# A prologue reordered: x and tables ahead of the weights, a mantissa converted on ScalarE, more of stage a between the two halves

## The chip, the cores and the metric

The kernel runs on one core of one Trainium2 chip. The metric is the device time of one execution in microseconds; the figure for a kernel is the median of several runs. A core has a matrix engine (TensorE, PE; its weight loads are PEld), VectorE (DVE), ScalarE (ACT), GpSimd (POOL), a sync engine (SP) that issues DMAs, and 16 DMA engines that all queues share.

## The reference

A Fourier layer, then a three-way maxout feed-forward layer, on x of 8 x 3072 x 256 (float32); the expert weights w1, w2, w3 (256 x 768) and w_out (768 x 256) come as float64.

```python
X = np.fft.rfft(x, axis=1)
Yr = X.real @ w_r - X.imag @ w_i + b_r
Yi = X.real @ w_i + X.imag @ w_r + b_i
Y = soft_threshold(Yr, 0.01) + 1j * soft_threshold(Yi, 0.01)
y = np.fft.irfft(Y, n=3072, axis=1).astype(np.float32).reshape(24576, 256)
h = np.maximum(np.maximum(y @ w1, y @ w2), y @ w3)
return (h @ w_out).astype(np.float32)
```

## The kernel before

The transform of 3072 points is split into 96 x 32. For each of the 8 batches, **stage a** multiplies a quad of x (`load_x`, `split_x`, `stage_a`; eight quads q to a batch, two matmuls pa each) by a 96-point table and writes the result, through tiles named aq, to a DRAM tile `a_d`. Twelve **blocks** k follow: `load_a` reads two rows of `a_d`, `stage_b` does the 32-point transform (px), `stage_w` multiplies by the complex weights (py) and adds the bias, a soft threshold comes next (uf, t), `finish_w` takes the maximum, `stage_q` does the first half of the inverse transform (pz) and writes zs to the DRAM tile `z_d`. Eight **chunks** c to a batch then read a piece of `z_d` (`load_z`, zq), split it into two float16 parts (`split_z`: zh on ScalarE, zl on VectorE), finish the inverse (`inverse`: pi, then yh and yl) and run the experts in six **slots** f: three `up` products (pu, each 6 float16 matmuls, combined by c on ScalarE and VectorE, h on VectorE, split into hh) and one `down` product (pd).

Batch 0 runs ahead of everything with float32 matmuls and on its own: eight quads of stage a, a loop over k from -3 to 12 with a hand-written plan of the weight work, and then the experts start. From there on the work of later batches is put between the slots of the experts by a list of positions in slots (`at`, `run_until`). Idle matmuls on zeros (`idle_matmuls`) fill PE's waits in the prologue.

The expert weights arrive as float64 and must become two float16 parts each. class `Weights` does that: `load` brings a pair of parts, `largest` takes the maximum of the high words, `scale` makes a power of two, and `phases` converts one part in three steps: exponent (a mask on VectorE, a Relu on ScalarE, L352 and L355), combine (four operations on VectorE, L359 to L367) and finish (the high part on ScalarE, two operations on VectorE, L126, L127 and L373). `w_up` has twelve parts of 128 x 384, `w_dn` six of 128 x 256. The plan of the loop takes the first six parts of `w_up` and three of `w_dn`; the others are `units`, of which `pump` moves each running one by a phase and starts one more. Pumps stand at k = 9 to 12 and five after each slot of the first chunk. `split_fft_weights` takes the maxima of the FFT weights and of the bias, makes their scales and splits them into float16 (L271 to L296), in program order after slot 2 of the first chunk; `largest_x` does not exist yet, the maxima of x (mxx, L444) are in `split_x`.

The program is ordered at build time: each engine gets one fixed list of instructions, chosen among those whose inputs should be there, the earlier in the program first. `tc.issue_after(ins)` adds an edge: what is traced inside it stands behind `ins` on that engine's list. `raw_tile` gives one of eight large buffers, `ff_tile` one of eight PSUM banks in turn, `quad_tile("aq")` one of two.

## Time and profile before

| | |
|---|---|
| runs | 2041.36, 2042.45, 2044.10 us; median 2042.45 |
| profiled execution | 2041.44 us, of which the span of the trace 2039.6 us |
| PE busy | 2016.9 us (99%) |
| PEld, DVE, ACT, POOL busy | 1413.9, 1447.3, 1032.3, 24.3 us |
| PE's part of the chain that ended last | 89%; DMA 4%, DVE 4% |

A busy PE includes its idle matmuls and the time at a lower granted clock. The chain is followed back from the last instruction to what released each step.

### The profile page before, as it was taken

The page shows a single profiled execution, that of the slowest core. Times are in us where ns is not written, and L with a number is a line of the kernel's source. Part 1 is how long each engine was busy: PE and PEld are TensorE (multiplying, and loading weights), DVE is VectorE, ACT ScalarE, POOL GpSimd, SP SyncE. Part 2 cuts the span into 40 slices and gives each one's busy share as a digit, 9 for nine tenths or more (in the row PEclk, how much of TensorE's full clock was granted, in tenths as well). Part 3 has the DMA queues.
Part 4 walks back from the last instruction along what each step waited for, and adds up shares of the span by engine and source line. Part 5 has one row for each costly group of instructions (what it writes and reads, how often), then busy time and mean ns, then how long its engine had stood idle before and what let it go on. Part 6 is the DMA issues. An engine that isn't in the chain of part 4 may idle for free.

```text
span 2039.6 us, 40089 instructions
## 1 busy us (share of the span) xinstructions
PE 2016.9 (99%) x15836; PEld 1413.9 (69%) x15836; DVE 1447.3 (71%) x2813; ACT 1032.3 (51%) x2050; POOL 24.3 (1%) x81
## 2 busy tenths in 40 slices
PE   8999999999999999999999999999999999999999
PEld 4756776677776777677776777767777677776666
DVE  3997886678766877668776777767876677755544
ACT  4756554455544554445554555545554455533333
POOL 1000000000000000000000000000000000000000
PEclk9999999999999999999999999999999999999999
DMA  9455542434333442434434344243441423211100
GB/s 312 149 160 140 141 119 86 119 99 124 93 103 84 120 115 72 125 80 123 105 95 113 81 120 104 80 117 98 109 111 47 117 73 100 66 53 32 40 24 24
DMA packets 199535, 207.74 MB, mean 102 GB/s; under 512 B 20131, under 2 KB 177827, under 8 KB 199251
## 3 DMA queue, kind: packets, MB, share of 16 engines
q1 hardware_dynamic: 138371, 129.20, 24.8%
q10 hardware_dynamic: 59744, 72.11, 11.1%
q0 software_dynamic: 1232, 3.87, 0.6%
q8 instruction: 124, 2.03, 0.4%
q14 instruction: 64, 0.52, 0.1%
HBM read 87.40 MB, written 75.50 MB: 80 GB/s over the span
## 4 chain that ended last, share of the span: by engine, by line
PE 89%; DMA 4%; DVE 4%; ACT 1%; issue 1%; SPq 0%; ACTq 0%; DVEq 0%
PE pu L159 17%; PE pu L160 17%; PE pu L161 17%; PE pd L161 6%; PE pd L160 6%; PE pd L159 6%; PE py L159 3%; PE py L161 3%; PE py L160 3%; PE px L586 2%; DMA ab<-a_d 1%; PE pa L161 1%; PE pa L160 1%; PE pa L159 1%; DMA zq<-z_d 1%; PE pi L161 1%
## 5 line engine op out<-in xcount | busy, mean ns | idle before, releaser
L159 PE MATMUL pu<-yh,wuh 128*128 128x384 f16 x2304 | 751.1, 326 | 6.0 <-ACT c L814 3.2
L160 PE MATMUL pu<-yl,wuh 128*128 128x384 f16 x2304 | 750.6, 326 | 0.9 <-DVE yl L154 0.7
L161 PE MATMUL pu<-yh,wul 128*128 128x384 f16 x2304 | 750.7, 326 | 0.0
L153 ACT ACTIVATE hh<-h 128x384 f16<-128x384 f32 x384 | 200.4, 522 | 530.8 <-DVE h L820 529.1
L817 DVE TENSOR_TENSOR c<-pu,c 128x384 f32<-128x384 f32 x384 | 211.9, 552 | 180.5 <-ACT c L814 93.7
L161 PEld LDWEIGHTS <-wul 128*128 128x128 f16 x2304 | 225.2, 98 | 150.9 <-issue 2.0
L159 PEld LDWEIGHTS <-wuh 128*128 128x128 f16 x2304 | 225.4, 98 | 130.5 <-issue 11.7
L160 PEld LDWEIGHTS <-wuh 128*128 128x128 f16 x2304 | 225.5, 98 | 130.0 <-issue 11.5
L161 PE MATMUL pd<-woh,hh 128*128 128x256 f16 x1152 | 313.7, 273 | 0.2 <-DVE ebf L294 0.2
L160 PE MATMUL pd<-wol,hh 128*128 128x256 f16 x1152 | 313.9, 273 | 0.0
L159 PE MATMUL pd<-woh,hh 128*128 128x256 f16 x1152 | 313.9, 273 | 0.0
L154 DVE SCALAR_TENSOR_TENSOR hh<-h,hh 128x384 f16<-128x384 f32 x384 | 213.1, 555 | 122.1 <-ACT hh L153 121.7
L814 ACT ACTIVATE c<-pu 128x384 f32<-128x384 f32 x384 | 185.8, 484 | 142.2 <-PE pu L161 123.4
L820 DVE TENSOR_TENSOR h<-pu,c 128x384 f32<-128x384 f32 x384 | 212.3, 553 | 57.9 <-PE pu L161 50.6
L159 PE MATMUL py<-wch,tt 128*128 128x256 f16 x504 | 137.4, 273 | 0.0
L161 PE MATMUL py<-wch,tt 128*128 128x256 f16 x504 | 137.3, 273 | 0.0
L160 PE MATMUL py<-wcl,tt 128*128 128x256 f16 x504 | 137.3, 272 | 0.0
L160 PEld LDWEIGHTS <-hh 128*128 128x128 f16 x1152 | 112.7, 98 | 33.4
L159 PEld LDWEIGHTS <-hh 128*128 128x128 f16 x1152 | 112.7, 98 | 33.4
L849 ACT ACTIVATE o<-pd,s1u 128x256 f32<-128x256 f32 x191 | 82.6, 466 | 82.2 <-PE pd L161 41.0
L161 PEld LDWEIGHTS <-hh 128*128 128x128 f16 x1152 | 112.7, 98 | 13.6 <-DVE ebf L294 0.5
L154 DVE SCALAR_TENSOR_TENSOR zl<-zq,s0u,zh 96x1024 f16<-96x1024 f32 (+1 forms) x65 | 81.9, 1262 | 31.8 <-ACT zh L153 31.8
(204 smaller groups left out, 2686.9 us busy)
## 6 DMA issues: line engine op xcount, KB each, us to landing
z_d<-zs ACTq DMA_DIRECT2D x96, 256.0 KB, 2.2
out_dram<-o ACTq DMA_DIRECT2D x190, 128.0 KB, 2.1
zq<-z_d SPq DMA_DIRECT2D x63, 384.0 KB, 4.1
xq<-in_x_dram SPq DMA_DIRECT2D x58, 384.0 KB, 4.1
a_d<-aq ACTq DMA_DIRECT2D x56, 384.0 KB, 3.3
ab<-a_d SPq DMA_DIRECT2D x84, 256.0 KB, 3.9
ab<-ab SPq DMA_DIRECT2D x336, 64.0 KB, 2.1
vb<-vb SPq DMA_DIRECT2D x308, 64.0 KB, 2.4
```

Source lines behind the costliest of these rows:

```text
L153: nc.scalar.activation(out=hi, in_=src, func=AF.Copy, scale=scale)
L154: later(lambda: nc.vector.scalar_tensor_tensor(out=lo, in0=src, scalar=scale, in1=h, op0=ALU.mult, op1=ALU.subtract))
L159: nc.tensor.matmul(o, lh, rh, start=start, stop=False, **kw)
L160: nc.tensor.matmul(o, lh, rl, start=False, stop=False, **kw)
L161: st["mm"] = nc.tensor.matmul(o, ll, rh, start=False, stop=stop, **kw)
L586: nc.tensor.matmul(pv[:, h, :, g // 2, g % 2], ah[:, g // 2, g % 2, h * P:(h + 1) * P], mb_sb[:, i, 4 * kb + g].rearrange("p (c m) -> p c ...
L814: nc.scalar.activation(out=c1, in_=p, func=AF.Copy)
L817: nc.vector.tensor_tensor(out=c1, in0=p, in1=c1, op=ALU.max)
L820: nc.vector.tensor_tensor(out=h32, in0=p, in1=st["c1"], op=ALU.max)
L849: nc.scalar.activation(out=o, in_=pd[t], func=AF.Copy, scale=st[b, "su"][1])
```

## The change

The order of loads in the prologue: x first, then two blocks of the table `mb_f`, and only behind the first read of `a_d` the FFT weights, the other blocks, the bias, `qf` and `id_sb` (on SP's queue, where they were on POOL's), then the expert weights, each one step of k later. `phases` works on a pair of parts at once and in four steps: the mantissa word goes through a ScalarE Relu (scale 2^-20, bias 1), the low word is added and the result multiplied by the power of two, so that VectorE has six operations for what took seven. The scales of the FFT weights move to k = 0 of the loop, their split stays after slot 2 but behind an edge. Quads 8 to 12 (before: 8 and 9) of x are loaded in the loop and go through stage a before the first inverse; their maxima are put at positions 1 to 3 of the slots. The pumps after the loop, the maxima and the split stand behind edges (`quiet`). Idle matmuls: 34 and 4 in place of 32 and 16.

```diff
+    EARLY = NCH + 5
 def load_fft_weights():
-        rows = [b.rearrange("(o d) -> o d", o=1) for b in (b_r, b_i)]
-        nc.gpsimd.dma_start(out=qf, in_=mq[:, 0:2])
-        for j in range(2):
-            for c in range(2):
-                nc.gpsimd.dma_start(
-                    out=bias[64 * c:64 * c + 64, j, :], in_=rows[c].broadcast_to([64, D])
-                )
-        nc.gpsimd.dma_start(out=bias[96:97, 1, :], in_=rows[0])
+    def load_tables():
+        rows = [b.rearrange("(r o d) -> r o d", r=1, o=1) for b in (b_r, b_i)]
+        for c in range(2):
+            nc.sync.dma_start(out=bias[64 * c:64 * c + 64], in_=rows[c].broadcast_to([64, 2, D]))
+        nc.gpsimd.dma_start(out=bias[96:97, 1:2], in_=rows[0])
+        nc.sync.dma_start(out=qf, in_=mq[:, 0:2])
+        nc.sync.dma_start(out=id_sb, in_=ident)
...
             def exponent():
-                e = x_tile("xh").bitcast(U32)[:, 0:width]
-                t["g"] = g = x_tile("xl").bitcast(U32)[:, 0:width]
+                g = x_tile().rearrange("p a b -> p (a b)")[:, 0:pair * width].bitcast(U32)
+                t["g"] = g = g.rearrange("p (k v) -> p k v", k=pair)
                 nc.vector.tensor_scalar(
-                    out=e, in0=hw, scalar1=0x7FF00000, scalar2=None, op0=ALU.bitwise_and
+                    out=g, in0=hw, scalar1=0x7FF00000, scalar2=None, op0=ALU.bitwise_and
                 )
-                nc.scalar.activation(out=g, in_=e, func=AF.Relu, scale=8.0, bias=ebias)
+                nc.scalar.activation(out=g, in_=g, func=AF.Relu, scale=8.0, bias=ebias)
             def combine():
...
                 nc.vector.tensor_scalar(
-                    out=hw, in0=hw, scalar1=12, scalar2=9, op0=ALU.logical_shift_left,
-                    op1=ALU.logical_shift_right,
+                    out=hw, in0=hw, scalar1=0xFFFFF, scalar2=None, op0=ALU.bitwise_and
                 )
-                nc.vector.tensor_tensor(out=hw, in0=hw, in1=g, op=ALU.bitwise_or)
+                nc.scalar.activation(out=m, in_=hw, func=AF.Relu, scale=2.0**-20, bias=ones)
+
+            def join():
                 nc.vector.scalar_tensor_tensor(
-                    out=r, in0=lw, scalar=2.0**-52, in1=g.bitcast(F32), op0=ALU.mult, op1=ALU.mult
+                    out=m, in0=lw, scalar=2.0**-52, in1=m, op0=ALU.mult, op1=ALU.add
                 )
+                nc.vector.tensor_tensor(out=m, in0=m, in1=t["g"].bitcast(F32), op=ALU.mult)
             def finish():
-                split_scaled(hi, m, m, self.sc)
-                nc.vector.scalar_tensor_tensor(
-                    out=lo, in0=r, scalar=self.sc, in1=m, op0=ALU.mult, op1=ALU.add
-                )
+                split_scaled(hi, lo, m, self.sc)
...
 def load_x(q):
-        with tc.issue_after(st["ld"].ins) if q >= NCH + 2 else nullcontext():
-            if 2 <= q < NCH:
+        with tc.issue_after(st["ld"].ins) if q >= EARLY else nullcontext():
+            if 2 <= q < NCH or NCH + 2 <= q < EARLY:
                 xq = raw_tile("xr")[0:N1, 0:NQ * D]
+    def largest_x(q, i, xp):
+        b, q4 = divmod(q, NCH)
+        with tc.issue_after(quiet[0]) if q < EARLY else nullcontext():
+            nc.vector.tensor_reduce(
+                out=batch(b, "x")[0:N1, 2 * q4 + i:2 * q4 + i + 1], in_=xp, axis=AX.X,
+                op=ALU.max, apply_absolute_value=True,
+            )
 def split_x(q):
+            if q >= EARLY:
+                largest_x(q, i, xp)
+            elif b:
+                at(1 + q4 / 2, lambda u: largest_x(*u), (q, i, xp))
...
-    load_first_blocks(0)
-    fft_weights = load_fft_weights()
+    load_first_blocks(0, 2)
...
-    idle_matmuls(32)
-    nc.gpsimd.dma_start(out=id_sb, in_=ident)
+    idle_matmuls(34)
     def prepare(w, n):
-        phase(w, n)
-        phase(w, n)
+        for _ in range(3):
+            phase(w, n)
-    for n in range(12):
-        if n % 2 == 0:
-            planned(-3 + n // 2, w_up.load, n)
+    for n in range(0, 12, 2):
+        planned(-2 + n // 2, w_up.load, n)
         planned(-2 + n // 2, w_up.largest, n)
-    for n in range(6):
-        planned(-1 + n, prepare, w_up, n)
+    for n in range(0, 6, 2):
+        planned(n, prepare, w_up, n)
         planned(5 + n // 2, phase, w_up, n)
...
         with tc.issue_after(st["ld"].ins):
+            if k == -3:
+                fft_weights = load_fft_weights()
+                load_first_blocks(2, 4)
+            if k == -2:
+                load_tables()
+            if k == 0:
+                scale_fft_weights(fft_weights)
+                split_scaled(*(t.rearrange("p a b -> p (a b)") for t in (qh, ql, qf)), Q_SCALE)
...
-            if k in (7, 8):
+            if 7 <= k < 12:
                 load_x(NCH + k - 7)
             if k == 9:
-                units += [(w_up, n) for n in range(6, 12)] + [(w_dn, n) for n in range(3, 6)]
-            if k >= 9:
+                units += [(w_up, n) for n in (6, 8, 10)] + [(w_dn, n) for n in (3, 4)]
+            if k in (9, 10):
                 pump()
-    for q in (NCH, NCH + 1):
+    with tc.issue_after(st["late"].ins):
+        for c, v in enumerate((b_r, b_i)):
+            row = v.rearrange("(o d) -> o d", o=1)
+            nc.gpsimd.dma_start(out=bias_ri[:, c], in_=row.broadcast_to([P, D]))
+    quiet = st["power"].ins, st["zs"].ins
+    def pumps(n):
+        with tc.issue_after(quiet[0]), tc.issue_after(quiet[1]):
+            for _ in range(n):
+                pump()
+    pumps(1)
+    for q in range(NCH, EARLY):
         split_x(q)
         stage_a(q)
-    idle_matmuls(16)
+    idle_matmuls(4)
     load_z(0, 0)
     split_z(0, 2)
     y = inverse(0, 0)
+    quiet = st["low"].ins, st["zs"].ins
...
-                    for _ in range(5):
-                        pump()
+                    pumps(5)
                     if f == 2:
-                        split_fft_weights(fft_weights)
+                        with tc.issue_after(quiet[0]):
+                            split_fft_weights(fft_weights)
```

Here `st["power"]` is the last operation of `power`, `st["zs"]` the last zs and `st["low"]` the last low part that `split_later` made with a scale.

## Rows read from the trace of the kernel before

**Rows 1.** The page's first part: busy time of PE, share of the span, instructions.

```profile
PE 2016.9 (99%) x15836; PEld 1413.9 (69%) x15836; DVE 1447.3 (71%) x2813; ACT 1032.3 (51%) x2050; POOL 24.3 (1%) x81
```

**Rows 2.** Busy time by stretch: the stretch in us from the span's start, its length, busy us (and instructions) of PE, PEld, DVE, ACT and POOL, granted PE clock, share of the 16 DMA engines, GB/s.

```profile
5.10:22.10 17.00, 15.37 (x36) 5.39 (x36) 1.11 (x2) 9.33 (x17) 4.73 (x10) 1.00 1.03 280
...
31.90:97.20 65.30, 64.20 (x313) 52.91 (x314) 60.42 (x151) 41.89 (x80) 0.96 (x3) 0.97 0.66 226
97.20:112.70 15.50, 12.71 (x61) 6.17 (x60) 14.35 (x40) 9.36 (x17) 0.00 (x0) 0.89 0.59 186
112.70:141.30 28.60, 27.39 (x177) 16.21 (x177) 28.12 (x76) 17.98 (x37) 0.00 (x0) 1.00 0.41 124
...
165.00:2039.60 1874.60, 1863.08 (x15072) 1314.79 (x15069) 1323.15 (x2494) 940.81 (x1878) 13.57 (x56) 1.00 0.35 93
```

**Rows 3.** The timeline of the head: start, duration, engine, line, operation, out<-in, count, and in brackets the idle time before it with its releaser.

```profile
5.13 4.33 PE L462 MATMUL pa<-xq,fr 96*96 96x512 f32 x8
...
11.96 0.52 POOL L225 DMA_DIRECT2D bias<-in_b_r_dram  x1 [6.19 <-DMA bias<-in_b_i_dram]
...
21.65 7.07 PE L870 MATMUL idle<-zeros 128*128 128x512 f16 x32
...
22.73 0.51 POOL L466 DMA_DIRECT2D a_d<-wuh  x1 [1.21 <-ACT wuh L465]
...
28.97 0.37 SPq L490 DMA_DIRECT2D aj<-a_d  x1
...
31.90 1.13 PE L524 MATMUL px<-mb_all,aj 128*128 128x128 f32 x8 [3.18 <-DMA aj<-a_d]
```

**Rows 4.** DMA issues of the first 120 us: what, engine, count, KB each, median us from issue to landing.

```profile
wst<-in_w_r_dram SPq DMA_DIRECT2D x1, 256.0 KB, 17.4
...
qf<-in_dft_ib_dram POOLq DMA_DIRECT2D x1, 128.0 KB, 5.9
bias<-in_b_r_dram POOLq DMA_DIRECT2D x2, 64.0 KB, 7.1
```

**Rows 5.** Three pieces of the chain that ended last, inside the loop: start, time, what.

```profile
41.29 0.89 PE px L524 x8
42.18 0.43 PE py L552 x2
...
44.34 0.86 PE pz L567 x2
```

**Rows 6.** Stretches, as in Rows 2; the second is PE alone.

```profile
31.90:37.50 5.60, 4.91 (x21) 4.17 (x22) 2.72 (x7) 1.99 (x4) 0.00 (x0) 0.70 1.03 392
...
34.00:35.00 1.00, 1.00 (x3) 0.50 1.07 412
```

**Rows 7.** The timeline of the pause.

```profile
97.64 0.68 DVE L555 TENSOR_TENSOR uf<-py,bias 128x512 f32<-128x512 f32 x1
...
101.39 1.35 PE L570 MATMUL pz<-uf,qf 128*128 128x256 f32 x4 [1.66 <-DVE uf L559]
...
108.75 1.32 ACT L153 ACTIVATE zh<-zq,s0u 96x512 f16<-96x512 f32 x2
...
110.29 1.41 DVE L154 SCALAR_TENSOR_TENSOR zl<-zq,s0u,zh 96x512 f16<-96x512 f32 x2
...
112.68 0.65 PE L159 MATMUL pu<-yh,wuh 128*128 128x384 f16 x3 [0.41 <-ACT yh L153]
```

**Rows 8.** The timeline of the first chunk.

```profile
113.75 0.60 DVE L127 SCALAR_TENSOR_TENSOR rw<-rw,swu,wuh 128x384 f32<-128x384 f32 x1
...
114.28 0.55 DVE L359 SCALAR_TENSOR_TENSOR xl<-rw,xl 128x384 uint32<-128x384 uint32 x1
...
114.75 0.61 DVE L373 SCALAR_TENSOR_TENSOR wul<-rw,swu 128x384 f16<-128x384 f32 x1
...
122.74 0.55 DVE L817 TENSOR_TENSOR c<-pu,c 128x384 f32<-128x384 f32 x1
...
123.34 0.32 PE L159 MATMUL pu<-yh,wuh 128*128 128x384 f16 x1 [0.29 <-DVE c L817]
...
125.46 0.42 DVE L367 SCALAR_TENSOR_TENSOR rw<-rw,xl 128x256 f32<-128x256 uint32 x1
125.80 0.42 DVE L366 TENSOR_TENSOR rw<-rw,xl 128x256 uint32<-128x256 uint32 x1
...
139.13 0.55 DVE L820 TENSOR_TENSOR h<-pu,c 128x384 f32<-128x384 f32 x1
```

**Rows 9.** Time from issue to landing of the `a_d` writes: those of the first 40 us (POOL's queue), then, from 100 to 240 us, those on ScalarE's queue with the reads of `a_d`.

```profile
DMA to landing us min/median/max: 2.8/8.6/10.7
...
DMA to landing us min/median/max: 2.7/3.9/6.0
```

**Rows 10.** Single operations: two neighbours on VectorE in the timeline, four splits of the FFT weights in one row, and two groups of ScalarE by line (count, busy us, mean ns, idle before).

```profile
107.84 0.35 DVE L352 TENSOR_SCALAR xh<-rw 128x384 uint32<-128x384 uint32 x1
108.11 0.14 DVE L253 TENSOR_SCALAR s1u<-s1u 128x1 uint32<-128x1 uint32 x1
...
131.05 1.66 DVE L127 SCALAR_TENSOR_TENSOR wcl<-wst,sc,wch 128x256 f16<-128x256 f32 x4
...
L557 ACT ACTIVATE t<-uf,mlam 128x512 f32<-128x512 f32 x11 | 7.9, 718 | 2.4 <-DVE uf L555 2.4
...
L355 ACT ACTIVATE xl<-xh,ebias 128x384 uint32<-128x384 uint32 x9 | 5.3, 611 | 4.3 <-DVE xh L352 4.3
```

More of the change, by code (lines that the diff above doesn't have):

```diff
@@ L252, in power @@
         nc.vector.tensor_scalar(out=t, in0=t, scalar1=255.0, scalar2=None, op0=ALU.min)
-        nc.vector.tensor_scalar(out=t, in0=t, scalar1=23, scalar2=None, op0=ALU.logical_shift_left)
+        st["power"] = nc.vector.tensor_scalar(
+            out=t, in0=t, scalar1=23, scalar2=None, op0=ALU.logical_shift_left
+        )
         return t.bitcast(F32)
@@ L275, in split_fft_weights @@
         st["lim", "x"] = limits("x", e, 142.0)
-        sc = power("sc", e, -1.0, 267.0, 1)
+        st["sc"] = power("sc", e, -1.0, 267.0, 1)
+        mb = small("mxb")
+        nc.vector.tensor_reduce(
+            out=mb, in_=bias.rearrange("p j d -> p (j d)"), axis=AX.X, op=ALU.max,
+            apply_absolute_value=True,
+        )
+        st["eb"] = small("ebf")
+        nc.vector.tensor_scalar(
+            out=st["eb"], in0=exponent_of(mb, "b", 23, 0xFF, 60.0), scalar1=1.0, scalar2=-37.0,
+            op0=ALU.mult, op1=ALU.add,
+        )
+    def split_fft_weights(ws):
+        sc = st["sc"]
         for kd, t in enumerate(ws):
@@ L286, in split_fft_weights @@
             split_scaled(wch[:, kd, 3], wcl[:, kd, 3], s, sc)
-        split_scaled(*(t.rearrange("p a b -> p (a b)") for t in (qh, ql, qf)), Q_SCALE)
-        mb = small("mxb")
-        nc.vector.tensor_reduce(
-            out=mb, in_=bias.rearrange("p j d -> p (j d)"), axis=AX.X, op=ALU.max,
-            apply_absolute_value=True,
-        )
-        st["eb"] = small("ebf")
-        nc.vector.tensor_scalar(
-            out=st["eb"], in0=exponent_of(mb, "b", 23, 0xFF, 60.0), scalar1=1.0, scalar2=-37.0,
-            op0=ALU.mult, op1=ALU.add,
-        )
     mlam = small("mlam")
@@ L305, in fourier_maxout_kernel, with __init__ @@
     nc.vector.memset(ebias, -896.0 * 2.0**23)
+    ones = small("ones")
+    nc.vector.memset(ones, 1.0)
     class Weights:
-        def __init__(self, name, parts, both):
-            self.name, self.parts, self.raw, self.both = name, parts, {}, both
+        def __init__(self, name, parts):
+            self.name, self.parts, self.raw = name, parts, {}
             self.mx = fft.tile([P, len(parts)], F32, name="mw" + name, bufs=1)
         def load(self, n, homes=None):
-            src = [self.parts[n + i][2] for i in range(2)]
-            width = src[0].shape[1]
+            width = 2 * self.parts[n][0].shape[1]
             if homes:
@@ L458, in stage_a @@
         for i, xp in enumerate(st.pop(("xs", q))):
-          with tc.issue_after(st["gate"]) if q >= NCH + 2 and q < NATIVE else nullcontext():
+          with tc.issue_after(st["gate"]) if EARLY <= q < NATIVE else nullcontext():
             pa = ff_tile("pa")
@@ L537, in first_b @@
             st["ts"] = s_tile("tsf").rearrange("p (h m) -> p h m", h=KD)
-            nc.gpsimd.tensor_copy(out=st["ts"], in_=t[:, :, 192:320])
+            st["late"] = nc.gpsimd.tensor_copy(out=st["ts"], in_=t[:, :, 192:320])
             for z in (32, 96):
@@ L730, in stage_q @@
         zs = fft.tile([P, 2, D], F32, name="zs")
-        nc.scalar.activation(out=zs, in_=pv, func=AF.Copy, scale=st[b, "sv"][1] if b else 1.0)
+        st["zs"] = nc.scalar.activation(
+            out=zs, in_=pv, func=AF.Copy, scale=st[b, "sv"][1] if b else 1.0
+        )
         nc.scalar.dma_start(out=rows_of(b, "z", kb), in_=zs)
@@ L903, in fourier_maxout_kernel @@
     planned(6, w_dn.load, 4)
-    for n in range(6):
-        planned((4, 4, 5, 5, 7, 7)[n], w_dn.largest, n)
+    for k, n in ((4, 0), (5, 2), (5, 3), (7, 4)):
+        planned(k, w_dn.largest, n)
     planned(7, w_dn.scale)
-    for n in range(3):
-        planned(5 + n, prepare, w_dn, n)
-        planned(8 + n, phase, w_dn, n)
+    for k, n in ((5, 0), (7, 2)):
+        planned(k, prepare, w_dn, n)
+        planned(k + 3, phase, w_dn, n)
     for k in range(-3, NJP + 1):
```

89 lines of the change are left out of this document (45 added, 44 removed).

## The prediction

> **What bounds the kernel now.** I read the page's shares first. TensorE is busy for all but 22.7 us of the span and VectorE for 71% [rows 1]. From 165 us on PE is busy for 99.4% of the time [rows 2]. The change does not touch that part, so whatever it does happens before 165 us. By stretch [rows 2], the head has five stages, and I looked in each for the wait that ends last.
>
> *Stage a of batch 0, to 22.1 us.* PE starts on x at 5.13 [rows 3]. It has 32 records (two for each of 16 fp32 matmuls) that follow each other at 0.43 us, 13.8 us in all, yet idle matmuls only take over at 21.65. So about 2.8 us are waits for x. The 16 DMA engines are full (share 1.03), and besides x they carry the tables that POOL asked for at 1.3 to 5.8 us, 0.13 MB of `qf`, four `bias` loads, two of `bias_ri` and `id_sb`, 0.7 MB [rows 2, 4].
>
> *The turn through DRAM, to 31.9 us.* The last `a_d` write is issued at 22.73, the first read back at 28.97, the first px matmul runs at 31.90 [rows 3]. The idle matmuls last only to 28.7.
>
> *The loop over 12 blocks, 31.9 to 97.2 us.* PE is busy for 64.2 of 65.3 us, VectorE for 60.4, ScalarE for 41.9 [rows 2]. A block is 8 px records at 0.11, 16 py records at 0.216, and 2 pz records at 0.43 us (by start to start) [rows 5]: 5.2 us, so 61.6 us for 12 blocks less the last pz. Of the other 3.7 us, 1.7 come from the clock: 34 to 37.3 us was granted half the rate, 1.2 in place of 2.4 GHz, two microseconds after PE's idle stretch [rows 6].
>
> *The pause, 97.2 to 112.7 us.* A chain with one link on each engine: uf, two Relus, pz, zs, out to `z_d`, back to zq, zh, zl, pi, yh, first pu matmul at 112.68 [rows 7].
>
> *The first chunk, 112.7 to 141.3 us.* VectorE is busy for 28.1 of 28.6 us, PE for 27.4 [rows 2]. The weight conversions go ahead of the expert network's own operations: c of slot 1 runs at 122.74, 10 us after the first pu matmul, and PE then waits for it [rows 8]. VectorE is the bound here, and PE hides that with stage a of later quads (5 x 2 matmuls).
>
> **The change, part by part.** The sum is made against the profiled execution, 2041.44 us (span 2039.6 plus 1.84 around it), which lies 1.0 us below the median of 2042.45.
>
> *x first.* `qf`, four `bias` loads and `id_sb` leave POOL's queue for SP's, behind the first block of a; `wst` and four of the six `mb` blocks go there too, and `bias_ri` waits until the end of the loop. POOL's wait of 6.19 us at the fifth `bias` load [rows 3] no longer stands ahead of the `a_d` writes. PE then runs stage a at its own pace: 5.13 + 13.8 = 18.9, or 2.8 us sooner. The last `a_d` write landed 6.2 us after its issue, and such writes take from 2.8 us [rows 9]; with 1.5 MB less in the queues (0.7 MB of POOL's tables, 0.5 of `wst`, 0.3 of `mb`) I take 4.0, nearer the lower, for 2.2 us more. That makes 5.0 us and puts px at 26.9. The idle matmuls set a floor: 34 of them at 0.216 us end at 26.3. Bounds: 2.8 (only the pace) to 5.6 us (the floor).
> What is moved past: behind the read of block 0 SP now issues two `wst`, one `mb`, one read of a, two `bias`, `qf`, `id_sb`, another `mb` and only then expert weights, at about 0.4 us each [rows 3]. `wst`, 0.5 MB, at the 392 GB/s of that stretch [rows 6] takes 1.4 us behind block 0 and is needed 1.6 us after it (px, then tf). I cost it at nothing; what hides it is px and tf, and without that cover it is the rival below. Expert weights come one step later; VectorE has nothing else to do with them until block 0.
>
> *The clock.* With px at 26.9 and idle matmuls to 26.3 the gap of 3.2 us is gone. I count 1.6 of the 1.7 us (bounds 0 and 1.7).
>
> *Conversion.* Start to start, a two-input operation of 384 elements takes 0.47 us and one of 256 takes 0.34; a mask of 384 takes 0.27 (about 0.2 for 256); those with a per-partition scale 0.53 and 0.40 [rows 8, 10]. So 768 elements take 0.86, 0.50 and 0.91 by the same slopes. A pair of `w_up` parts went through 2 x (2 x 0.27 + 3 x 0.47 + 2 x 0.53) = 6.0 us; now it takes 2 x 0.50 + 3 x 0.86 + 0.91 = 4.5. Six pairs save 9.2 us, `w_dn` in the same way 3.2: 12.4 us of VectorE. In the loop this is worth nothing, since PE sets its pace. ScalarE gets one more Relu per pair, about 0.9 us by its 0.61 for 384 elements [rows 10]: at 41.9 of 65.3 us it has room. The Trainium skill (ScalarE: Activation LUTs, Rules for kernel authors) puts relu, add and multiply on VectorE, which it calls up to three times faster; here the two engines take 0.61 and 0.55 us for such an operation, and by the rule the mantissa would stay on VectorE, the saving would be 12.4 less 6 x 0.86 and 1.9 for `w_dn`, 5.3 us, and the loop would be as long.
>
> *Exponents of the FFT weights and the bias* move into the loop (k = 0), with two pt matmuls of two records and their turns in PSUM: +0.7 us (0 to 1.5).
>
> *The pause.* The x maxima and all conversion are now held behind `power` and zs, and after inverse(0, 0) behind the last yl. That ordering removes what stood in the chain: about 1.1 us between py and pz (97.2 to 101.39, 4.2 us, where uf at 0.68, two Relus at 0.72, uf and the hand-overs need 3.1 [rows 7, 10]), 0.8 between zh and zl, 0.4 in pz, whose four records took 1.35 in place of 0.9. Three more quads of stage a go here, 6 matmuls of 0.86 us, where 12 idle matmuls go out: PE has 10 x 0.86 + 2.2 us of work in 13 us, so it fits. But their `a_d` writes share ScalarE's DMA queue with the last `z_d`, and aq has two buffers; I charge 0.75 us. Sum -1.5 (bounds -3 and +3, one write of 2.7 us or more ahead of `z_d` [rows 9]).
>
> *The first chunk.* Stage a of three quads (5.2 us) has left it, so PE would be that much shorter here. VectorE is not. The loop's plan now converts six `w_up` parts and three of `w_dn`; two pumps in the loop and one in the pause advance units 6, 8 and 10, and the rest may start only behind yl: 0.91 + (1.72 + 0.91) + (0.86 + 0.50 + 1.72 + 0.91) + 1.8 + 3.1 = 12.5 us. Ten x maxima at 0.6 us (512 elements, as uf, less the overlap) and the split of the FFT weights (8 x 0.40 + 4 x 0.34 = 4.6) come behind the same edge. With c, h, hh, zl and yl up to h of slot 4 (8.3 us) it is 31.4 us from 1.0 us after the first pu matmul; before, h of slot 4 ended 26.9 us after it [rows 8]. So VectorE is 5.5 us later relative to its start. PE is ahead at that point by one more matmul of stage a (0.9) and one down (0.9), and can fill its gap with stage a of quads 13 and 14, whose loads wait for the maxima of 8 and 9 (2.7 of 3.4). Net +1.0 (bounds -2, if all the gaps are filled, and +5.5).
>
> Sum: -5.0 - 1.6 + 0.7 - 1.5 + 1.0 = -6.4, so 2035.0 against the profiled execution and **2036.0** against the median.
>
> **Rivals.** *VectorE's debt takes the gain.* In the first chunk nothing fills PE; c of slot 1 comes 13 us after the first pu matmul, PE has work for 8, and the chunk gives back the full 5.5 us instead of 1.0: -1.9, 2040.5. For it: the order of the program is kept in that stretch [rows 8], and the maxima of x gate the loads. Such a gap can also cost clock, as after 28.7 us [rows 6]: up to 1.7 us more, 2042. The Trainium skill (TensorE: Matmul & The Clock Gate, HAM oscillation) says that matmuls after a wait run at the lower clock; by that rule, the trace at 34 us agrees.
> *More is won.* `a_d` turns at the floor, the pause gains its 3 us and the gaps are filled: -5.6 - 1.7 + 0.7 - 3 - 1 = -10.6, 2032. Against it: the extra writes in the pause.
> *Slower.* `wst` comes late. It landed 17.4 us after its issue when it stood behind x [rows 4]. Issued at 24 and landing at 41, py of block 0 starts 12.5 us later than I assume (28.5), which gives +6.1: 2048.6. It decides from a landing at 39 us on, where the 6.4 us are gone and 4.1 more are lost. Against it: block 0 is all that is ahead of it now.
>
> **Chances.** About 0.2% (4.1 us) can be told from no change. Forecast 0.5 (own range 2032 to 2040; of it 0.42 faster and 0.08 same), debt 0.25 (0.05 faster, 0.18 same, 0.02 slower), more won 0.12, all of it faster, late `wst` 0.13 (0.10 slower, 0.03 same). Faster 0.59, same 0.29, slower 0.12. The range goes from the third case with its last bounds (no loss in the loop, -2 in the chunk: 2030) to the debt with its clock and half of the pause's upper bound: 2030 to 2044.
>
> **What would show it.** Right: px at 26 to 28 us with the clock at 1.0, py of block 11 ending near 91, first pu matmul near 105, x maxima and conversions back to back on VectorE behind yl. Wrong: VectorE with gaps in the first chunk (then the debt is none), PE waiting there for c or h by more than 6 us (then it is larger), zq landing over 7 us after zs, or py of block 0 waiting for `wst`.

## The result, and the profile after

| | before | after |
|---|---|---|
| median of six runs each, on one chip | 2042.63 us (2039.47 to 2047.89) | 2055.58 us (2051.72 to 2058.14) |
| ratio, 95% interval | | 1.0061 [1.0045, 1.0077] |
| profiled execution, its span | 2041.44, 2039.6 us | 2055.69, 2053.9 us |

The change makes the kernel 13 us slower, where 2036.0 us was forecast and 2030 to 2044 us was the range. The page's first part and the stretches that answer to [rows 1, 2], columns as there:

```profile
PE 2020.9 (98%) x15826; PEld 1416.5 (69%) x15826; DVE 1436.6 (70%) x2740; ACT 1037.0 (50%) x2044; POOL 20.6 (1%) x75
```

```profile
5.10:22.10 17.00, 17.00 (x48) 6.64 (x49) 0.00 (x0) 9.47 (x16) 4.27 (x8) 1.00 1.01 324
...
97.20:120.20 23.00, 14.77 (x59) 6.54 (x59) 8.94 (x22) 11.27 (x20) 0.00 (x0) 0.85 0.63 195
120.20:155.20 35.00, 29.92 (x165) 16.87 (x165) 32.48 (x62) 18.89 (x33) 0.00 (x0) 0.85 0.23 68
```

VectorE does 10.7 us less in all, as it should. But the pause, from the end of the last py to the first pu, now takes 22.4 us in place of 15.5 and leaves every engine idle for a good part of it (PE for 8.2 of the 23.0 us, VectorE for 14.1), and the first chunk needs 35 us up to h of slot 4 in place of 27, both at a granted clock of 0.85.

Three places set the time. The timelines below have the columns of [rows 3].

**The head went as forecast.** The last `a_d` write was issued at 19.91 us, px started at 26.69 (forecast 26.9, before 31.90), and the first half of `wst` landed 3.0 us after its issue, the second by 29.1.

**The loop lost the whole lead.** The last py started at 97.24 us, before at 96.56. Timelines of POOL, then VectorE, then PE, and the row of POOL's bias load among the DMA issues:

```profile
19.91 0.51 POOL L489 DMA_DIRECT2D a_d<-wuh  x1 [1.21 <-ACT wuh L488]
33.99 0.49 POOL L228 DMA_DIRECT2D bias<-in_b_r_dram  x1 [13.57 <-DMA bias<-in_b_i_dram]
...
37.17 0.28 DVE L246 TENSOR_REDUCE ec<-pt 128x1 f32<-128x128 f32 x1
40.05 0.69 DVE L284 TENSOR_REDUCE mxb<-bias 128x1 f32<-128x512 f32 x1 [2.60 <-DMA bias<-in_b_r_dram]
40.66 0.14 DVE L247 TENSOR_SCALAR ec<-ec 128x1 uint32<-128x1 uint32 x1
40.77 0.15 DVE L239 TENSOR_REDUCE col<-mxb 128x1 f32<-128x1 f32 x1
...
41.40 0.68 DVE L582 TENSOR_TENSOR uf<-t,uf 128x512 f32<-128x512 f32 x1
...
26.69 1.13 PE L547 MATMUL px<-mb_all,aj 128*128 128x128 f32 x8 [0.35 <-DMA aj<-a_d]
...
31.14 1.78 PE L547 MATMUL px<-mb_all,aj 128*128 128x128 f32 x8 [1.35 <-DMA aj<-a_d]
...
40.98 0.49 PE L241 MATMUL pt<-id_sb,col 128*128 128x128 f32 x2 [2.51 <-DVE ec L250]
...
42.65 1.06 PE L574 MATMUL py<-wst,tf 128*128 128x256 f32 x2
```

```profile
bias<-in_b_r_dram POOLq DMA_DIRECT2D x1, 1.0 KB, 6.0
```

POOL loads one row of the bias (1 KB) over a row that SP's load of b_i writes first, so it waits for that load, is issued at 33.99 and takes another 6.0 us. VectorE's list is fixed: the bias maximum mxb, now at k = 0, waits until 40.05, and behind it stand col, which PE's next pt reads, two small operations on ec, uf of block 0 and all conversion. PE stands still for 2.5 us. Each of its two idle stretches is followed by half clock (two matmul records of py take 1.06 us at 42.65, 0.59 at full clock): the one from 38.5 to 41 us is the wait for the bias, the one from 29.8 to 31.1 lies ahead of it and is a wait for the read of block 1.

**The pause** answers to [rows 7]; ScalarE, then PE:

```profile
107.16 1.01 ACT L373 ACTIVATE rw<-rw,ones 128x768 f32<-128x768 uint32 x1 [2.07 <-DVE rw L370]
...
108.90 1.53 ACT L488 ACTIVATE aq<-pa 96x512 f32<-96x512 f32 x3
...
110.83 0.71 ACT L157 ACTIVATE zh<-zq,s0u 96x512 f16<-96x512 f32 x1
...
116.60 1.08 ACT L488 ACTIVATE aq<-pa 96x512 f32<-96x512 f32 x2 [5.06 <-DMA a_d<-aq]
117.57 0.71 ACT L157 ACTIVATE zh<-zq,s0u 96x512 f16<-96x512 f32 x1
...
118.34 0.26 PE L163 MATMUL pi<-ga_sb,zh 96*128 96x96 f16 x1 [5.45 <-ACT zh L157]
...
120.20 0.80 PE L163 MATMUL pu<-yh,wuh 128*128 128x384 f16 x2 [0.26 <-ACT yh L157]
```

The eviction of the fifth quad needs one of the two aq tiles and waits 5.06 us for the `a_d` write that empties it. The second half of zh is next on ScalarE's list, its input long there (in the version "both" below it runs 0.6 us behind the first half). That write is the third quad's, and it is late itself: the evictions of the third quad stand behind the mantissa's new Relu, which waits 2.07 us for VectorE.

**The first chunk** answers to [rows 8]; VectorE, then PE:

```profile
134.36 0.57 DVE L835 TENSOR_TENSOR c<-pu,c 128x384 f32<-128x384 f32 x1
...
132.25 0.28 PE L165 MATMUL pd<-woh,hh 128*128 128x256 f16 x1 [1.61 <-DVE hh L158]
134.98 0.48 PE L163 MATMUL pu<-yh,wuh 128*128 128x384 f16 x1 [2.01 <-DVE c L835]
```

c of slot 1 runs 14.2 us after the first pu (before 10.1), and PE waits for VectorE.

The difference to before, in profiled executions, runs like this: -5.2 us at px, +0.7 at the last py, +7.5 at the first pu, +15.5 at h of slot 4, +11.1 at h of slot 17, +14.3 at the end.

### The profile page after: what moved, and what is told of

Same layout as the page of the kernel before. It is cut to its first block, busy times and chain, and to the rows that moved or that the text cites. A ratio compares the mean times of both kernels' runs of the same rounds, so it can differ in the third digit from the quotient of the medians.

```text
span 2053.9 us, 39988 instructions
## 1 busy us (share of the span) xinstructions
PE 2020.9 (98%) x15826; PEld 1416.5 (69%) x15826; DVE 1436.6 (70%) x2740; ACT 1037.0 (50%) x2044; POOL 20.6 (1%) x75
## 4 chain that ended last, share of the span: by engine, by line
PE 89%; DMA 5%; DVE 3%; ACT 2%; issue 1%; SPq 1%; ACTq 0%; DVEq 0%; POOLq 0%
PE pu L163 17%; PE pu L164 17%; PE pu L165 17%; PE pd L164 6%; PE pd L163 6%; PE pd L165 6%; PE py L163 3%; PE py L164 3%; PE py L165 3%; PE px L609 2%; DMA zq<-z_d 1%; DMA ab<-a_d 1%; PE pi L165 1%; PE pa L165 1%; PE pa L163 1%; PE pa L164 1%
## 5 line engine op out<-in xcount | busy, mean ns | idle before, releaser
L163 PEld LDWEIGHTS <-wuh 128*128 128x128 f16 x2304 | 226.0, 98 | 129.8 <-issue 11.1
```

The lines of the kernel that those rows point to most:

```text
L163: nc.tensor.matmul(o, lh, rh, start=start, stop=False, **kw)
```

## The experiments

Each kernel was timed beside the kernel before on the same chip. In the series of the experiments the medians of before were 2046 to 2047 us, so its profiled execution (2041.44) is one of its quicker ones, and differences to its trace come out 1 to 8 us higher than the ratios say. Marks from the profiled executions, in us from the span's start: px, last py and first pu are where they start, h is where the operation ends, +/- against before; by slot 17 the quads that were moved are done in every kernel. A mark is that of one execution: px varies from 26.7 to 29.8 among the versions with the same new order of loads (all but "before" and "conversion alone").

| kernel | px | last py | first pu | c of slot 1 behind it | h of slot 4 | h of slot 17 | ratio, 95% interval |
|---|---|---|---|---|---|---|---|
| before | 31.9 | 96.6 | 112.7 | 10.1 | 139.7 | 205.0 | 1 |
| after | 26.7 | 97.2 | 120.2 | 14.2 | 155.2 | +11.1 | 1.0061 [1.0045, 1.0077] |
| bias late | 27.7 | 93.0 | 116.0 | 13.6 | 150.1 | +9.7 | 1.0018 [1.0007, 1.0030] |
| homes | 27.9 | 97.6 | 115.3 | 14.5 | 149.5 | +6.6 | 1.0025 [1.0011, 1.0038] |
| both | 27.7 | 92.7 | 109.9 | 14.6 | 144.8 | +2.4 | 0.9998 [0.9986, 1.0010] |
| two quads | 29.8 | 100.2 | 115.6 | 14.3 | 149.6 | +11.6 | 1.0038 [1.0022, 1.0055] |
| both, 2nd pump | 27.0 | 91.9 | 112.8 | 9.5 | 142.7 | -0.4 | 0.9991 [0.9979, 1.0003] |
| both, split later | 27.0 | 92.7 | 110.2 | 14.8 | 139.7 | +0.3 | 0.9978 [0.9965, 0.9991] |
| both, pump, split, idle | 26.9 | 92.4 | 113.4 | 9.8 | 138.3 | -1.4 | 0.9971 [0.9961, 0.9980] |
| both, idle | 27.3 | 92.2 | 109.5 | 14.8 | 144.3 | +0.8 | 0.9994 [0.9981, 1.0007] |
| **quads behind** | 27.4 | 92.3 | 110.5 | 8.9 | 135.4 | **-6.2** | **0.9955 [0.9942, 0.9968]** |
| quads behind, pump | 27.5 | 93.4 | 116.9 | 8.4 | 137.0 | -1.6 | 0.9982 [0.9972, 0.9993] |
| conversion alone | 31.5 | 97.2 | 113.8 | 7.7 | 134.0 | +0.4 | 0.9994 [0.9985, 1.0003] |
| head alone | 28.0 | 94.8 | 114.3 | 12.8 | 145.0 | +6.8 | 1.0018 [1.0006, 1.0030] |
| head, conversion | 28.1 | 94.7 | 111.0 | 8.4 | 133.6 | +1.2 | 0.9985 [0.9974, 0.9996] |
| quads behind, mantissa on VectorE | 27.4 | 93.7 | 111.8 | 11.7 | 137.6 | -1.5 | 0.9995 [0.9983, 1.0007] |

### The bias exponent later

```diff
+    def scale_bias():
         mb = small("mxb")
...
+            if k == 3:
+                with tc.issue_after(st["max"].ins):
+                    scale_bias()
```

> The changed kernel with one edit: the exponent of the bias (its maximum mxb and the pt matmul behind it) moves from k = 0 of the loop to k = 3, behind the threshold's maximum of that block. Theory (three separate losses: about 5 us in the loop behind the late bias load, 7 in the pause behind the two aq buffers, 5 to 8 in the first chunk from VectorE's debt, of which some 4 come back): the loop keeps its lead, PE is not idle at 41 us, last py of the loop starts at 92 to 94 us in place of 97.2, the first pu of the experts comes 3 to 5 us earlier than 120.2, and the ratio to the kernel before falls from 1.006 to about 1.004. Rival 1 (the lead is lost to the clock at 31 us and to the turn of the reads of a_d, the bias is harmless): last py stays at 96 us or later and the ratio at 1.006. Rival 2 (the pause waits for something that the loop does not set, such as the evictions of stage a): last py is early, but the first pu stays at 119 to 120 us, ratio 1.006.

The lead is kept: last py at 93.0 us, and no half clock before the pause. The 4.2 us are still there at the first pu. By the ratios the chain through the bias cost 8.8 us (1.0061 to 1.0018, where about 1.004 was expected), by the traces 5.0 at h of slot 4. The first of these ratios comes from another series, with before at 2042.63; between "homes" and "both" below, which were timed in one series and differ by this edit alone, it is 5.3 us (medians 2050.44 and 2045.10), and 4.9 at the last py. The half clock at 31 us is not the bias's: "homes" has the bias at k = 0 and none there (but at 41 us). The wait for the aq tile stands where it stood (ScalarE, 5.08 us).

### Homes for the quads

```diff
+        elif NCH + 2 <= q < EARLY:
+            i = 8 * (q - NCH - 2)
+            aq = mb_f[0:96, i:i + 8].rearrange("p k m -> p (k m)")
```

> The changed kernel with one edit: quads 10, 11 and 12 of stage a are evicted to space of the table mb_f that is free by then, so that none of the five in the pause waits for one of the two aq buffers. Theory (the fifth quad's eviction, waiting 5.1 us for its buffer on ScalarE, holds zh behind it): that wait is gone, both halves of zh start when zq has landed (by 109 to 111 us), the first pu comes at 112 to 114 us in place of 120.2, and the ratio goes from 1.006 to 1.002 to 1.003. Rival 1 (the transfers: a_d writes delay z_d or zq themselves, the buffer is no matter): zq lands late, zh half 2 still at 116 us or later. Rival 2 (VectorE's debt takes whatever the pause gives): the first pu is early, but h of slot 4 ends within 2 us of its old 155.2 us, ratio 1.005 to 1.006.

The wait is gone and the first pu comes 4.9 us sooner, less than the 6 to 8 expected, since zh now stands directly behind the last evictions. It stays gained at h of slot 4 (-5.7), so the debt did not eat it.

### Both

> Both edits together: the bias exponent at k = 3 and homes for quads 10 to 12. Theory (the two losses are separate and add): last py at 92 to 94 us, first pu at 107 to 110 us, h of slot 4 at 142 to 146 us in place of 155.2 (139.7 in the kernel before), ratio 0.999 to 1.002: the change then shows its gain in the head and its debt in the first chunk, and comes out about even. Rival (VectorE's debt is the one bound and has a fixed end): h of slot 4 stays at 150 us or later, ratio 1.004 or more.

All numbers as expected: the two losses are separate and add (10.3 us at h of slot 4, 5.0 + 5.7 alone). What is left is as fast as before, with the head's 4 us won and the first chunk's debt paid. ScalarE in its pause:

```profile
106.31 0.59 ACT L496 ACTIVATE mb_all<-pa 96x512 f32<-96x512 f32 x1
106.81 0.71 ACT L157 ACTIVATE zh<-zq,s0u 96x512 f16<-96x512 f32 x1
```

zh starts without a gap behind the tenth eviction: the pause is now bound by ScalarE's list, not by the transfer.

### Two quads in the pause

```diff
-    EARLY = NCH + 5
+    EARLY = NCH + 2
-            if 7 <= k < 12:
+            if k in (7, 8):
-    idle_matmuls(4)
+    idle_matmuls(16)
```

> The changed kernel with two quads of stage a in the pause as before, in place of five, and 16 idle matmuls in place of 4; the other three quads go back to the slots with their loads. Theory (the pause is long because of the three extra quads): no eviction stands before zh with a wait, first pu at 112 to 114 us; the three quads return to the first slots, where PE waits for VectorE anyway, so h of slot 4 ends 5 to 8 us earlier than 155.2, but the 4 us that were regained by slot 10 are no longer regained: ratio 1.003 to 1.005. Rival (the extra quads are a gain for PE, the pause is long for another reason): first pu at 118 us or later and the ratio above 1.006.

px came 3 us later in this run, in which stage a itself began later (first `a_d` write at 10.44 us in place of 7.91), which the edit does not touch. From the end of the last py the pause took 14.8 us in place of 22.4, but by the same reckoning h of slot 17 came only 2.5 us sooner: the three quads save in the slots most of what they cost in the pause, and the rival's half is true as well.

### The first chunk's debt: a second pump, a later split, idle matmuls

```diff
-    pumps(1)
+    pumps(2)
```

> The version with both edits (bias exponent at k = 3, homes for quads 10 to 12; ratio 0.9998 to the kernel before, h of slot 4 at 144.8 us) and one more: two pumps in place of one between the loop and the first inverse, so that six more conversion operations (4.2 us) run on VectorE in the 4.5 us in which it waited for zh. Theory (VectorE's debt is what PE waits for in the first chunk): c of slot 1 comes 10 to 11 us after the first pu matmul in place of 14.6, the half clock at 125 us goes, and h of slot 4 ends 3 to 5 us earlier (140 to 142 us); some of it is given back by slot 10, ratio 0.997 to 0.999. Rival (the first chunk's loss is PE's clock after the pause and the missing stage a, not VectorE): c of slot 1 earlier, but h of slot 4 within 1.5 us of 144.8.

```diff
-                        with tc.issue_after(quiet[0]):
-                            split_fft_weights(fft_weights)
...
+                if (b, c, f) == (0, 1, 1):
+                    with tc.issue_after(st["low"].ins):
+                        split_fft_weights(fft_weights)
```

> The version with both edits and one more: the split of the FFT weights into float16 (12 operations, 4.6 us on VectorE, as many on ScalarE) moves from slot 2 of the first chunk to slot 1 of the second, behind the last low part there. Theory (debt): c of slot 1 stays at 14.6 us after the first pu, h of slot 4 ends 3 to 5 us earlier than 144.8, and since by slot 7 VectorE has room, most of it stays: ratio 0.998 to 0.999. Rival 1 (VectorE has caught up by slot 4 anyway): h of slot 4 within 1 us of 144.8. Rival 2 (the gain of the regained stretch, slots 5 to 10, falls by as much): h of slot 10 within 1 us of 169.05, ratio 1.000.

```diff
-    pumps(1)
+    pumps(2)
-    idle_matmuls(4)
+    idle_matmuls(12)
```

(and the later split)

> The version with both edits, the second pump in the pause, the later split, and 12 idle matmuls in place of 4 ahead of the first inverse. Theory (three shares of one debt, and PE's clock): the first pu has the full clock, c of slot 1 at 10 to 11 us after it, h of slot 4 at 136 to 139 us (139.7 in the kernel before), ratio 0.996 to 0.998, faster than both kernels. Rival (they overlap: once PE is not waiting for VectorE, the chunk is bound by PE and the rest is lost): no better than the better one of the two, 0.998 or more.

```diff
-    idle_matmuls(4)
+    idle_matmuls(12)
```

> The version with both edits and 12 idle matmuls in place of 4 ahead of the first inverse. Theory (the half clock of 109 to 113 us comes from PE's idle stretch at 106 us): that half-rate stretch goes, h of slot 0 ends 1 to 2 us earlier than 115.4; VectorE then keeps c of slot 1 where it was, so h of slot 4 and the ratio hardly change (0.999 to 1.000). Rival (the clock is a loss by itself): the 1 to 2 us stay to the end. Rival 2 (idle matmuls stand ahead of pi and delay it): first pu later than 109.9 by up to 1.7 us.

The second pump brought c of slot 1 to 9.5 us (10 to 11 expected), but the first pu came 2.9 us later, so that h of slot 4 gained 2.1 us and not 3 to 5, and the ratio is not told from that of "both". ScalarE in that run:

```profile
106.51 0.97 ACT L375 ACTIVATE rw<-rw,ones 128x768 f32<-128x768 uint32 x1 [1.47 <-DVE rw L372]
...
107.78 1.06 ACT L496 ACTIVATE mb_all<-pa 96x512 f32<-96x512 f32 x2
...
109.24 0.71 ACT L157 ACTIVATE zh<-zq,s0u 96x512 f16<-96x512 f32 x1
```

The mantissa's new Relu waits for VectorE, and three evictions and zh wait behind it. The later split gave 5.1 us at h of slot 4 and kept 0.2% in the ratio (0.9998 to 0.9978, each to about 0.0013): the debt is real, and work that nothing needs yet should not be paid there. The idle matmuls restored the clock and nothing more; the stretch 108 to 112 us of "both" and of "both, idle" (length, PE busy, granted clock, DMA share, GB/s):

```profile
108.00:112.00 4.00, 3.27 (x27) 0.67 0.69 203
```

```profile
108.00:112.00 4.00, 3.48 (x35) 1.00 0.64 211
```

h of slot 0 ends 1.4 us sooner, h of slot 4 only 0.5. In the run with all three the clock fell again (half rate from 111 to 118 us), and zh was late by the pump (109.78 us): the shares don't add, and its 0.9971 can't be told from the 0.9978 of the later split alone.

### Two quads behind the first inverse

```diff
     for q in range(NCH, EARLY):
         split_x(q)
-        stage_a(q)
+        if q < NCH + 3:
+            stage_a(q)
...
     y = inverse(0, 0)
+    with tc.issue_after(st["pi"].ins):
+        for q in range(NCH + 3, EARLY):
+            stage_a(q)
```

(with both edits, the later split and 12 idle matmuls)

> The version with both edits, the later split and 12 idle matmuls, and one more: stage a of quads 11 and 12 stands behind the first inverse in place of ahead of it, so that zh waits on ScalarE behind six evictions of stage a in place of ten. Theory (the pause is bound by ScalarE's list: with both edits zh started 0.00 us after the last eviction and Relu, at 106.8): zh comes about 2 us sooner, at 104.5 to 105, first pu at 107 to 109 us in place of 109.5 to 110; PE does the four matmuls (3.4 us) where it waits for VectorE, so c of slot 1 still comes 14 us after the first pu, h of slot 4 ends at 134 to 137 us (136.6 to 139.7 before that edit), ratio 0.995 to 0.997. Rival (zq sets it: the transfer through DRAM lands at 106.5 anyway): first pu at 109 us or later, ratio 0.998 as without the edit.

ScalarE, then PE:

```profile
104.41 0.72 ACT L157 ACTIVATE zh<-zq,s0u 96x512 f16<-96x512 f32 x1
...
106.99 3.64 PE L493 MATMUL pa<-xr,fr 96*96 96x512 f32 x8
110.47 0.33 PE L163 MATMUL pu<-yh,wuh 128*128 128x384 f16 x1
```

zh starts at 104.41 us, 2.4 sooner than in "both". PE then runs the four matmuls ahead of the first pu, which is why that comes at 110.5 and not at 107 to 109, and why c of slot 1 is only 8.9 us behind it: VectorE works its debt off while PE does stage a. From 26 to 176 us the granted clock is 1.00 throughout (after: 0.92). At 2037.2 us beside 2046.1 this version beats both kernels. The version without this last edit (both edits, later split, 12 idle matmuls) was not run; the nearest are 0.9978 and 0.9994, so the edit's own share isn't measured by itself (0.23% against the better of these).

> The same with the second pump in the pause. Theory: with four evictions fewer ahead of zh ScalarE has room for the second pump's operations (a split of 1.0 us, a Relu of 1.0 and one of 0.5), which cost 3 us of pause when ten evictions stood there; first pu at 108 to 110 us, c of slot 1 at 10 to 11 us after it in place of 14, h of slot 4 at 132 to 136 us, ratio 0.993 to 0.996. Rival (ScalarE's order still puts a Relu that waits for VectorE ahead of zh, as in the run with the second pump alone): first pu at 111 us or later, no better than 0.997.

The same with `pumps(2)`, and the rival held. ScalarE and VectorE in the pause:

```profile
106.01 0.71 ACT L157 ACTIVATE zh<-zq,s0u 96x512 f16<-96x512 f32 x1
...
108.08 1.00 ACT L375 ACTIVATE rw<-rw,ones 128x768 f32<-128x768 uint32 x1 [1.36 <-DVE rw L372]
...
109.37 0.70 ACT L157 ACTIVATE zh<-zq,s0u 96x512 f16<-96x512 f32 x1
...
108.16 0.74 DVE L158 SCALAR_TENSOR_TENSOR zl<-zq,s0u,zh 96x512 f16<-96x512 f32 x1
```

The Relu that waits for VectorE went between the two halves of zh, and the second pump's operations ahead of zl.

### The parts alone

In the kernel before, the new class `Weights` and the plan by pairs:

```diff
+                nc.scalar.activation(out=m, in_=hw, func=AF.Relu, scale=2.0**-20, bias=ones)
...
-    for n in range(6):
-        planned(-1 + n, prepare, w_up, n)
+    for n in range(0, 6, 2):
+        planned(n, prepare, w_up, n)
```

> The kernel before with the new conversion alone (pairs, four steps, the mantissa through ScalarE); loads, tables, quads, pumps and idle matmuls as before. Theory (the conversion saves VectorE about 12 us, of which PE feels only the part in the first chunk, where VectorE is the bound): px at 31.9 and last py at 96 to 98 us as before, first pu within 1 us of 112.7, c of slot 1 and h of slot 4 1 to 4 us sooner after it than before (10.1 and 26.9 us), ratio 0.998 to 1.000. Rival 1 (the mantissa's Relus on ScalarE delay zh and the first chunk): first pu 1 to 3 us later and the ratio above 1.001. Rival 2: PE fills its gaps in the first chunk before and after, ratio 1.000.

In the kernel before, the new loads and the late bias:

```diff
-    load_first_blocks(0)
-    fft_weights = load_fft_weights()
+    load_first_blocks(0, 2)
...
+            if k == -3:
+                fft_weights = load_fft_weights()
+                load_first_blocks(2, 4)
+            if k == -2:
+                load_tables()
+            if k == 3:
+                with tc.issue_after(st["max"].ins):
+                    scale_bias()
```

> The kernel before with the new order of loads alone (x first, tables behind the first read of a_d, expert weights one step later, 34 idle matmuls) and the bias exponent at k = 3; conversion, quads and pumps as before. Theory (the head's gain is real and passes to the end when nothing new waits): px at 26.7 to 28 us in place of 31.9, no half clock at 34 us, last py at 91 to 93 us in place of 96.6, first pu at 107.5 to 109 in place of 112.7, h of slot 4 at 135 to 136.5 in place of 139.7, ratio 0.9975 to 0.9985. Rival (VectorE, 60 of 65 us busy in the loop with the weights one step later, gives the lead back): last py at 95 us or later, or c of slot 1 more than 12 us after the first pu, ratio 0.9995 or more.

Both of these in the kernel before:

> The kernel before with the new order of loads, the bias exponent at k = 3 and the new conversion; two quads in the pause, pumps and the FFT weights' split placed as before, no edges. Theory (the two parts need each other: with the weights one step later VectorE was busy without a gap from 40 to 104 us in the version with the head alone and gave the 3.9 us of lead back in the loop and the pause; the new conversion takes some 7 us from VectorE there): px at 27 to 28 us, last py at 92 to 94 us, first pu at 108 to 110 us in place of 114.3 (head alone) and 112.7 (before), h of slot 4 at 131 to 136 us, ratio 0.996 to 0.998. Rival 1 (the head's order costs by itself, by its loads): last py at 95 us or later, ratio 1.000 or more. Rival 2 (ScalarE's Relus take what VectorE gives): first pu 111 us or later.

The conversion alone is 5.7 us ahead at h of slot 4 and level by slot 7: PE had filled its waits for VectorE with stage a, and does that stage a later instead (ten records of it between the first pu and h of slot 4 in the kernel before, four here: 2.6 of the 5.7 us). The first chunk of the kernel before was bound by PE, in spite of VectorE's 28.1 of 28.6 us [rows 2].

The head alone was the surprise: 3.9 us ahead at px, and slower in the end. The stretch 40 to 100 us of before, of the head alone, and of "bias late" (all engines, columns as in [rows 2]), and PE in the loop and the pause of the head alone:

```profile
40.00:100.00 60.00, 59.32 (x286) 47.16 (x285) 59.13 (x146) 41.27 (x77) 0.96 (x3) 1.00 0.58 194
```

```profile
40.00:100.00 60.00, 56.47 (x268) 43.92 (x266) 59.32 (x151) 41.46 (x77) 0.53 (x3) 1.00 0.64 210
...
59.23 1.16 PE L526 MATMUL px<-mb_all,aj 128*128 128x128 f32 x8 [0.96 <-ACT tf L534]
...
100.81 2.07 PE L572 MATMUL pz<-uf,qf 128*128 128x256 f32 x4 [2.27 <-DVE lowu L262]
```

```profile
40.00:100.00 60.00, 59.28 (x282) 46.22 (x281) 52.66 (x114) 44.65 (x75) 1.55 (x5) 1.00 0.77 233
```

VectorE was full in both of the first two, but with the weights one step later its work was later against PE's: uf and the limits stood behind conversions, PE lost 2.9 us in the stretch. About half of that lies in the loop, as at 59.23, where px waits for ScalarE's tf. The rest lies ahead of pz of the last block, which waits 2.27 us (before: 1.66 [rows 7]); the row names lowu, but the uf that pz reads ended just ahead of it, at 100.76, behind conversions. With the new conversion in this order VectorE is still full (58.96 of 60), the loop no better (last py 94.7), but the pause 3.2 us shorter. So the conversion is worth about 1 us with the old order of loads (0.9994, not told from none) and about 7 us with the new one (1.0018 to 0.9985, intervals apart). The rest of the loop's loss goes only where the edges hold conversions and maxima back, as in "bias late": VectorE at 52.7 of 60 and last py at 93.0. That it is the edges and not the pumps' number was not tried apart.

### The mantissa on VectorE

```diff
-                nc.scalar.activation(out=m, in_=hw, func=AF.Relu, scale=2.0**-20, bias=ones)
+                nc.vector.tensor_scalar(
+                    out=m, in0=hw, scalar1=2.0**-20, scalar2=1.0, op0=ALU.mult, op1=ALU.add
+                )
```

(in the version with quads behind)

> The version of the run with quads 11 and 12 behind the first inverse (0.9955), with the mantissa's scale and bias on VectorE (one more operation with two constants, 0.50 us for 768 elements) in place of ScalarE's Relu (1.0 us). Theory (VectorE is the bound of the first chunk, ScalarE's list that of the pause): zh comes up to 1 us sooner, c of slot 1 and h of slot 4 0.5 to 2 us later relative to the first pu, for five conversions of 0.3 to 0.5 us; ratio 0.9955 to 0.9965. Rival (the Trainium skill's rule, ScalarE: Activation LUTs, Rules for kernel authors, that such an operation belongs on VectorE, counts here because ScalarE is the one that sets the pause): h of slot 4 1 us or more earlier, ratio 0.9945 to 0.995.

Slower by more than expected (0.9955 to 0.9995). The stretch 50 to 60 us of the version with the Relu, then of this one, with PE's wait in it:

```profile
50.00:60.00 10.00, 9.99 (x53) 8.08 (x52) 10.00 (x23) 6.50 (x12) 0.00 (x0) 1.00 1.05 355
```

```profile
50.00:60.00 10.00, 8.48 (x49) 7.13 (x48) 10.00 (x17) 5.08 (x9) 0.00 (x0) 1.00 0.99 344
...
59.52 0.49 PE L241 MATMUL pt<-id_sb,col 128*128 128x128 f32 x2 [1.47 <-DVE col L239]
```

VectorE is full in both. With the mantissa on it the bias maximum comes later on its list (col at 59.33 us, with the Relu at 57.10), and PE's pt waits 1.47 us for it. c of slot 1 moves from 8.9 to 11.7 us, and the half clock is back (122.8 to 126.4 us). The rule of the Trainium skill that puts such an operation on VectorE (ScalarE: Activation LUTs, Rules for kernel authors) does not hold for this kernel, in which VectorE is the fuller engine: the measurement decides. The factor of three that the prediction quotes stands there for bf16; the operations here are in float32 and uint32.

## Why the prediction was wrong, step by step

*x first: right.* -5.2 us at px against -5.0; the rival of a late `wst` did not happen. That it fits to 0.2 us is luck: the same head gave -2.1 to -5.0 us in the profiled executions of the other versions.

*The loop (+0.7, the clock -1.6): wrong by 6.6 us.* The forecast had the last py 5.9 us earlier, it was 0.7 later. The step counted the moved exponents as two pt matmuls and their turns. It did not follow what they read: SP's load of b_i, POOL's load behind it, mxb on VectorE, and the uf and pt behind mxb in VectorE's fixed list. The prediction named the bias loads as moved past and did not ask who waits for the last. That chain cost 4.9 us at the last py ("homes" against "both"), the second stretch of half clock included. The other 1.7 us are the clock's step: the gap ahead of px was gone, but behind waits of 0.69 and 1.35 us at blocks 0 and 1 half the rate was granted from 31.4 to 35.0 us all the same. In 12 of the 14 profiled executions with this head it was not, so that in this step the forecast failed in the execution profiled and not in general; what decides between them stays open.

*Conversion, "in the loop this is worth nothing": right for the old order of loads, wrong for the new.* The 12.4 us of VectorE are what keeps the new order from losing, about 7 us by the runs. "ScalarE has room" holds for the loop; in the pause the new Relu, waiting for VectorE, holds up evictions and zh. And with the mantissa on VectorE the loop would not be as long: its last py starts 1.4 us later.

*The pause (-1.5, bounds -3 and +3): wrong by 8.3 us*, outside its own bounds. "aq has two buffers" stood in the text, at 0.75 us together with the writes. The price is the third use of a tile: the fifth quad's eviction waits until the third quad's write has landed, 5.06 us, on the engine that runs zh next. The upper bound took one write ahead of `z_d` and left out an eviction ahead of zh. PE's work was summed there (it fits) and ScalarE's list was not: with the wait for the tile gone ("homes") the pause is still 3.1 us longer than forecast.

*The first chunk (+1.0, bounds -2 and +5.5): right in kind, under-sized.* c of slot 1 at 14.2 us was forecast by the rival as 13, h of slot 4 at 35.0 us as 32.4; half clock from 133.9 to 140.7 us is part of the rest. Some 4.3 us came back by slot 17, since three quads are gone from there: +3.6 in all. The later split and the quads behind the inverse take this loss away.

*Later ("whatever it does happens before 165 us"): wrong in the traces.* +3.2 us between slot 17 and the end were not forecast, and they arise in one place, between slots 50 and 60 (+3.6). A maximum of x waits there on VectorE's list for its load, with yl and c behind it, and PE waits for these. VectorE and PE of the kernel before:

```profile
395.29 0.68 DVE L444 TENSOR_REDUCE mxx<-xq 96x1 f32<-96x512 f32 x1 [3.58 <-DMA xq<-in_x_dram]
...
399.54 0.32 PE L159 MATMUL pu<-yh,wuh 128*128 128x384 f16 x1 [1.71 <-DVE c L817]
```

And after, with PE's half clock behind it (columns as in [rows 2]):

```profile
408.24 0.68 DVE L456 TENSOR_REDUCE mxx<-xq 96x1 f32<-96x512 f32 x1 [4.25 <-DMA xq<-in_x_dram]
...
409.90 0.32 PE L164 MATMUL pu<-yl,wuh 128*128 128x384 f16 x1 [1.32 <-DVE yl L158]
412.49 0.32 PE L163 MATMUL pu<-yh,wuh 128*128 128x384 f16 x1 [2.10 <-DVE c L835]
...
413.60:417.20 3.60, 3.60 (x17) 2.21 (x15) 2.48 (x5) 1.21 (x3) 0.00 (x0) 0.53 0.30 67
```

PE waits 3.4 us in place of 1.7, and some 3.4 us at half clock cost another 1.7 by estimate. The wait stands in both kernels; half clock follows it in 6 of the 15 changed versions, and not in the one profiled execution of before. Whether the change makes it likelier isn't shown, and some of the 3.2 us may be no loss of the change.

So 6.6 + 8.3 + 2.6 + 3.2 = 20.7 us lie between the forecast of -6.4 and +14.3 in the traces. With the two waits mended the kernel is level with before (0.9998): what the head won, the first chunk takes. Only with the later split, the idle matmuls and the two quads behind the inverse, none of them part of the forecast, does it come to 0.9955, next to the forecast's 0.9968; that the figures are near is no proof of the forecast.

## What to carry to other kernels

When an operation is moved forward, follow each of its inputs back to the last transfer and its issue, and read on its engine's list what then stands behind it. When work is added in a wait, sum it for every engine and count the uses of each buffer: here the fifth quad in two buffers waited 5 us for a whole transfer, and ScalarE's fixed order made the next, unrelated operation pay. An engine that is full but hidden is no bound, as "conversion alone" shows; it became one when its inputs came later, as "head alone" shows. A wait that is there before the change can grow after it: look past the part that the change touches.

## What the runs showed of the hardware

- A load of 1 KB on POOL's queue, issued at 33.99 us, took 6.0 us to land, as long as loads of 128 KB that SP had issued 6 to 8 us earlier (5.2 to 6.3 us); the share of the 16 DMA engines was 1.05 from 34 to 40 us and 0.90 from 26 to 34.
- Waits of PE cost twice here. In after, half clock followed the idle stretches at 29.8, 38.5 and 111 us and the waits at 132 and 410 us; two stretches, columns as for "both, idle":

```profile
116.00:120.00 4.00, 1.32 (x12) 0.50 0.49 162
136.00:140.00 4.00, 4.00 (x16) 0.50 0.27 71
```

In the first PE had little to do and it cost little, in the second it was busy throughout.
